# Queries turned by one transposing DMA instead of six fp32 TensorE products, for 12 of 16 head pairs

## The chip, the cores and the metric

The kernel runs on one core of a Trainium2 chip. The metric is the device time of one execution in microseconds (us); lower is better. Before the change it is 271.0 us, the median of three runs (269.58 to 273.28).

## The reference, cut to what matters

Two layers follow each other. The first is a block-sparse causal attention (4 batches, 8 heads, 768 positions, 64 wide): each query picks three key blocks of 64 by a gate score against the mean key of each block, and its own block. The second is a gated convolution over the sequence, done by FFT in the reference. Only the parts that the change touches are shown in full.

```python
# q, k, v: (4, 8, 768, 64) float32
k_rep = k.reshape(B, H, n_blocks, 64, D).mean(axis=3)
gate_scores = np.einsum('bhsd,bhnd->bhsn', q, k_rep)      # chooses the blocks
gate_scores = np.where(causal, gate_scores, -1e9)
top_idx = np.argsort(gate_scores, axis=-1)[..., -3:]       # plus the own block
scores = np.matmul(q, k.transpose(0, 1, 3, 2)) / np.sqrt(D)
attn = softmax(where(chosen_blocks & causal, scores, -1e9))
x = (attn @ v) as (4, 768, 512)

x1, x2, x3 = split(x @ w_proj)                             # 512 wide each
y = x1 * irfft(rfft(x2) * rfft(filter)) * x3
out = y @ w_out
```

The choice of blocks compares gate scores with each other, so it needs queries that are more exact than one rounding to 16 bits. The score product is content with the rounded ones.

## The kernel before

**Tiling.** Two heads of one batch form a pair `p` (0 to 15): 128 partitions of head dimension. The sequence is 6 chunks of 128. A pair has 6 slots of work, 3 per head, so there are 96 slots; pair `p` begins at slot `n0 = 6p`. In each slot the loop at L700 records, in this order: `scores` of the next slot (TensorE), `exponentials` of this slot (ScalarE, then a causal cut on GpSimd), the transfers gathered in `late` (`flush`), the list `early[n]`, a share of the second layer of the batch before (`hyena`), `products` of the slot before, and the list `bank[n]`. The schedule is written out by hand: every engine runs its instructions in the order in which they are recorded, and a waiting instruction holds all behind it on its engine. SyncE (SP) issues nearly all DMAs, also in that order, and it too stands still while one waits.

**What the queries need.** Their two heads are loaded side by side as fp32, positions on partitions (`q_nat`, three buffers). The products need them turned: 128 head dimensions on partitions, 768 positions along the row. Per pair `prep_q` (L325) is called twice, at slots `n0 - 9` and `n0 - 8`, each time for three chunks:

- `turned_pair` (L282): three fp32 products with an identity turn three chunks into a PSUM tile `qt` (L285). These tiles come from a pool of three (`one`), which most of the second layer's products use too.
- ScalarE rounds `32 q` to fp16 into `TQ` (L333). VectorE takes what the rounding left, `32 q - TQ`, as fp16 into `ql` (L335), without the first chunk, which needs no gate.
- After the second call a DMA copies the lower half of `TQ`, the second head, to `QB` (L339), as the score products of that head want it on partitions 0 to 63.

**Who uses them.** `prep_gate` (slot `n0 - 7`, L344 and L350): a bias product, then per chunk `TQ` twice and `ql` once against the two parts of the mean keys, 15 small products. `prep_mask` finds the third largest (VectorE). `prep_turn` (slot `n0 - 5`) turns the mask, ScalarE scales it (L383, tile `m`), and two DMAs put its rows at partitions 64 to 75 of `TQ` and `QB` (L385, L386), where the score product adds them. `scores` (L407) reads `TQ` with `KA` for the first head, `QB` with `KB` for the second.

**The other transfers of a pair on SP.** Loads of keys (`k_nat`, slot `n0 - 17`), queries (`n0 - 13`) and values (`n0 - 8`); the turned keys' halves to `KA` and `KB` (L307, L308); outputs (L576); and, for the second layer, one transposing DMA per pair from pair 4 on, except each batch's last pair (L455): it turns the attention's result `xnat`, six chunks of 128 x 128 in fp16, into `xT`.

**The second layer's inverse transform** keeps a tile `yy` per 128 channels (L544, four buffers).

Of the kernel before, what the change touches and what calls it, by code (L numbers as in the profile page):

```python
# [9 lines left out]
FP32 = mybir.dt.float32  # L10
FP16 = mybir.dt.float16
BF16 = mybir.dt.bfloat16
AF = mybir.ActivationFunctionType
ALU = mybir.AluOpType
# [4 lines left out]
def kernel(  # L19
# [10 lines left out]
    nc = tc.nc  # L30

    B, H, S, D = q.shape
    P = 128
    SC = S // P
    NB = S // 64
    Dm = H * D
    DC = Dm // P
    N3 = 3 * Dm
    F = 384
    HC = F // P  # L40
    NP = B * DC
    QS = 32.0
# [7 lines left out]
    fp = FP16  # L50
# [3 lines left out]
    const = ctx.enter_context(tc.tile_pool(name="const", bufs=1))  # L54
# [17 lines left out]
    nats = {}  # L72
# [94 lines left out]
    V16 = [const.tile([P, SC, 2, 66], fp, name=f"V16_{i}") for i in range(3)]  # L167
    KA = [const.tile([P, S], fp, name=f"KA{i}") for i in range(2)]
    KB = [const.tile([P, S], fp, name=f"KB{i}") for i in range(3)]
    TQ = [const.tile([P, S], fp, name=f"TQ{i}") for i in range(2)]  # L170
    QB = [const.tile([P, S], fp, name=f"QB{i}") for i in range(2)]
    id16 = const.tile([P, P], fp, name="id16")
    ownm = const.tile([P, SC - 1, 2, NB], fp, name="ownm")
# [150 lines left out]

    def prep_q(p, t):  # L325
        qn = nats["q", p]
        tq = TQ[p % 2]
        if t == 0:
            state["ql", p] = hp.tile([P, S], fp, name="ql", tag="ql")
        ql = state["ql", p]  # L330
        qt = turned_pair("qt", qn, t)
        cols = slice(F * t, F * (t + 1))
        nc.scalar.activation(tq[:, cols], qt, AF.Copy, bias=0.0, scale=QS)  # L333
        lo = P if t == 0 else 0
        nc.vector.scalar_tensor_tensor(out=ql[:, F * t + lo:F * (t + 1)], in0=qt[:, lo:F],  # L335
                                       scalar=QS, in1=tq[:, F * t + lo:F * (t + 1)],
                                       op0=ALU.mult, op1=ALU.subtract)
        if t == 1:
            late.append(lambda: nc.sync.dma_start(QB[p % 2][0:D, :], tq[D:P, :]))  # L339

    def prep_gate(p):
        tq, ql, kr = TQ[p % 2], state.pop(("ql", p)), state.pop(("kr", p))
        g = one("g", (P, SC - 1, 2, NB))
        nc.tensor.matmul(g.rearrange("p c h n -> p (c h n)"), lhsT=half1,  # L344
                         rhs=biasr.rearrange("p c h n -> p (c h n)"),
                         start=True, stop=False, skip_group_check=True)
        for c in range(1, SC):
            sl = slice(P * c, P * (c + 1))
            for lhs, rhs, last in ((tq, 0, False), (tq, 1, False), (ql, 0, True)):
                nc.tensor.matmul(g[:, c - 1], lhsT=lhs[:, sl], rhs=kr[:, rhs],  # L350
                                 start=False, stop=last, skip_group_check=True)
        state["g", p] = g
# [125 lines left out]
    def hyena(b, spread):  # L478
# [53 lines left out]
        def inverse(dc):  # L532
# [8 lines left out]
                                 start=(j == 0), stop=(j == HC - 1))  # L541
            yes = hy2.tile([P, F], FP32, name="yes", tag="yes")
            nc.scalar.copy(yes, ye)
            yy = hy.tile([P, 2, F], FP32, name="yy", tag="yy", bufs=DC)  # L544
            nc.vector.tensor_add(yy[:, 0, :], yes, yo)  # L545
            nc.vector.tensor_sub(yy[:, 1, :], yes, yo)  # L546
            st["y", dc] = yy
# [91 lines left out]
    def at(where, n, f):  # L639
        if n < slots:  # L640
            where[max(n, 0)].append(f)

    def gate_mask(p):
        prep_gate(p)
        prep_mask(p)

    for p in range(NP):
        n0 = 2 * NS * p
        k_at = {1: (0, 0), 2: (3, 3)}.get(p, (n0 - 12, n0 - 10))
# [2 lines left out]
        t_at = {1: 4, 2: 8}.get(p, n0 - 5)  # L652
        if p > 2:
            at(early, k_at[0] - 5, lambda p=p: load(p, "k"))
            at(early, q_at[0] - 4, lambda p=p: load(p, "q"))
        if p > 1:
            at(early, n0 - 8, lambda p=p: load(p, "v"))
        if p:
            for t in range(2):
                at(bank, k_at[t], lambda p=p, t=t: prep_k(p, t))  # L660
                at(bank, q_at[t], lambda p=p, t=t: prep_q(p, t))
            at(early, max(k_at[1] + 1, q_at[1]), lambda p=p: prep_kr(p))
            at(bank, g_at, lambda p=p: gate_mask(p))
            at(bank, t_at, lambda p=p: prep_turn(p))
            at(early, n0 - 3, lambda p=p: prep_v(p))
# [113 lines left out]
```

## Time and profile before

| | |
|---|---|
| median of three runs | 271.0 us (269.58 to 273.28) |
| the profiled execution | 272.46 us, its span 270.7 us, mean granted TensorE clock 0.979 |
| busy share of the span | TensorE 89%, VectorE 66%, ScalarE 63%, GpSimd 52% |
| fp32 products that turn the queries (L285) | 96, 17.4 us busy |
| rounding to `TQ` (L333) and the rest `ql` (L335) | 32 of 15.7 us and 32 of 15.5 us in total |
| transposing DMAs of `xnat` (L455) | 9 |
| DMA | 36.29 MB, 134 GB/s on the mean |

The span is what the profile covers, from the first to the last instruction; the 1.76 us around it belong to the time. Busy times of a group count overlapping instructions once. TensorE's products overlap each other by their latency, so a row of three products is busy for longer than it keeps the next one waiting. The profile's slices are 6.8 us each.

### The profile page before, as it was taken

Reading aid. Unit: us, or ns where it says so; the run is one execution under the profiler, and the core shown is the slowest. Engines: PE = TensorE matmul, PEld = TensorE weight load, DVE = VectorE, ACT = ScalarE, POOL = GpSimd, SP = SyncE. Lnnn points to the kernel's source line nnn. Section 1 sums busy time; section 2 is a strip of 40 time slices with the busy share of each in tenths; the row PEclk is TensorE's granted clock in tenths of the full one; section 3 lists DMA queues with packets and bytes.
Section 4 is the critical chain, followed back from the end, with each engine's and each line's share of the span. In section 5 each row is a group of like instructions: output and inputs, shape, how many; then the busy total and the mean of one; then the engine's idle time right before and its main releaser. Section 6 shows DMA issues by size and latency. Waiting matters only on the chain.

```text
span 270.7 us, 6236 instructions
## 1 busy us (share of the span) xinstructions
PE 242.0 (89%) x2228; PEld 150.3 (56%) x2228; DVE 179.1 (66%) x550; ACT 171.4 (63%) x275; POOL 140.9 (52%) x260
## 2 busy tenths in 40 slices
PE   7696869996999999989999999899999989897874
PEld 3365735565665667655656676566655654443431
DVE  3568658889477988654569885725698663256680
ACT  4567766774767577769764777797756756342333
POOL 7513342689635778653236876714277872006540
PEclk9999979997699999999999999999999999999999
DMA  8997977889797855677665467767241044200006
GB/s 162 209 153 208 245 205 140 157 162 212 128 190 159 155 124 131 125 210 232 150 134 121 106 150 105 190 212 195 59 93 37 1 33 155 77 2 0 0 0 232
DMA packets 93654, 36.29 MB, mean 134 GB/s; under 512 B 84292, under 2 KB 89784, under 8 KB 93624
## 3 DMA queue, kind: packets, MB, share of 16 engines
q1 hardware_dynamic: 91368, 33.81, 54.9%
q0 software_dynamic: 2256, 2.10, 5.9%
q8 instruction: 17, 0.28, 0.5%
q14 instruction: 13, 0.11, 0.2%
HBM read 24.64 MB, written 6.29 MB: 114 GB/s over the span
## 4 chain that ended last, share of the span: by engine, by line
PE 58%; DVE 15%; ACT 10%; POOL 6%; issue 4%; DMA 3%; SPq 1%; POOLq 0%; DVEq 0%; ACTq 0%
PE sps L407 8%; PE x2p L495 7%; PE op L572 6%; PE o L437 5%; PE x3p L560 5%; ACT ex L416 5%; PE x1p L557 4%; PE mt L371 2%; PE kt L285 2%; PE qt L285 2%; PE warm L92 2%; PE sps L557 2%; DVE xnat L446 2%; PE sps L560 2%; PE g L350 2%
## 5 line engine op out<-in xcount | busy, mean ns | idle before, releaser
L416 ACT ACTIVATE ex<-sps 128x896 f16<-128x896 f32 x96 | 88.3, 926 | 3.3 <-PE sps L407 3.0
L419 POOL TENSOR_SCALAR_AFFINE_SELECT ex<-ex 128x256 f16<-128x256 f16 x96 | 40.4, 424 | 82.6 <-ACT ex L416 78.3
L437 PEld LDWEIGHTS <-ex 128*128 128x128 f16 x672 | 32.7, 99 | 26.3 <-DVE xnat L446 11.6
L437 PE MATMUL o<-V,ex 128*128 128x65 f16 x672 | 37.5, 196 | 5.8 <-DVE xnat L446 4.4
L407 PE MATMUL sps<-QB,KB 76*128 76x512 f16 (+1 forms) x144 | 27.0, 297 | 3.7 <-ACT ex L416 3.6
L407 PE MATMUL sps<-TQ,KA 76*128 76x512 f16 (+1 forms) x144 | 27.4, 302 | 1.9 <-DMA QB<-m 1.3
L518 POOL TENSOR_TENSOR PQ<-ta 128x512 f16<-128x512 f32 x12 | 15.2, 1270 | 23.8 <-DVE ta L517 23.8
L572 PE MATMUL op<-wo,yT 128*128 128x512 f16 x96 | 24.2, 379 | 3.0 <-POOL yT L527 3.0
L301 DVE TENSOR_REDUCE krs<-kt 128x6 f32<-128x384 f32 x32 | 17.5, 553 | 13.5 <-ACT KH L298 13.3
L495 PE MATMUL x2p<-wp,xf 128*128 128x512 f16 x96 | 24.3, 379 | 0.8 <-DVE xf L474 0.8
L298 ACT CAST KH<-kt 128x384 f16<-128x384 f32 x32 | 15.2, 481 | 13.9 <-PE kt L285 12.6
L333 ACT ACTIVATE TQ<-qt 128x384 f16<-128x384 f32 x32 | 15.7, 495 | 12.3 <-PE qt L285 12.1
L335 DVE SCALAR_TENSOR_TENSOR ql<-qt,TQ 128x256 f16<-128x256 f32 (+1 forms) x32 | 15.5, 485 | 11.7 <-ACT TQ L333 11.6
L565 DVE TENSOR_TENSOR gg<-x1sb,x3p 128x384 f32<-128x384 f16 x24 | 13.2, 551 | 12.7 <-ACT x1sb L563 7.9
L527 POOL TENSOR_TENSOR yT<-gg,yy 128x384 f16<-128x384 f32 x16 | 15.9, 997 | 10.4 <-DVE yy L545 10.3
L575 ACT COPY osb<-op 128x512 f32<-128x512 f32 x24 | 14.1, 587 | 10.8 <-PE op L572 9.2
L560 PE MATMUL x3p<-xT,wp 128*128 128x384 f16 x96 | 19.6, 326 | 0.5 <-DVE yy L546 0.5
L407 PEld LDWEIGHTS <-KB 76*128 76x128 f16 x144 | 13.6, 100 | 11.0 <-issue 5.6
L557 PE MATMUL x1p<-xT,wp 128*128 128x384 f16 x96 | 19.5, 326 | 0.0
L383 ACT ACTIVATE m<-mt 44x768 f16<-44x768 f16 x14 | 11.3, 805 | 12.6 <-PE mt L371 12.6
L446 DVE TENSOR_TENSOR xnat<-o,rc 128x384 f16<-128x384 f32 x32 | 17.8, 558 | 1.1
L359 DVE MAX8 m<-g 128x8 f32<-128x12 f32 x160 | 13.9, 161 | 6.8 <-PE g L350 6.8
(155 smaller groups left out, 498.0 us busy)
## 6 DMA issues: line engine op xcount, KB each, us to landing
q_nat<-in_q_dram SPq DMA_DIRECT2D x32, 192.0 KB
k_nat<-in_k_dram SPq DMA_DIRECT2D x32, 192.0 KB
v_nat<-in_v_dram SPq DMA_DIRECT2D x32, 192.0 KB
out_dram<-osb SPq DMA_DIRECT2D x24, 256.0 KB
QB<-TQ SPq DMA_DIRECT2D x16, 96.0 KB
KA<-KH SPq DMA_DIRECT2D x16, 96.0 KB
KB<-KH SPq DMA_DIRECT2D x16, 96.0 KB
wp<-in_moe_w_proj_dram POOLq DMA_DIRECT2D x12, 128.0 KB, 3.8
```

The costliest lines, as they stand in the source:

```text
L301: nc.vector.tensor_reduce(out=krs[:, 6 * t:6 * t + 6], in_=kt.rearrange("p (n j) -> p n j", j=64), axis=AX.X, op=ALU.add)
L333: nc.scalar.activation(tq[:, cols], qt, AF.Copy, bias=0.0, scale=QS)
L407: nc.tensor.matmul(t[:, col:col + q1 - q0], lhsT=kk[0:64 + NB, P * kc:P * (kc + 1)], rhs=qq[0:64 + NB, q0:q1], start=True, stop=True, skip ...
L416: nc.scalar.activation(ex, t[:, 0:W], AF.Exp, bias=0.0, scale=EXPS)
L419: nc.gpsimd.affine_select(out=tri, in_=tri, compare_op=ALU.is_ge, fill=0.0, base=0, pattern=[[0, 2], [1, P]], channel_multiplier=-1)
L437: nc.tensor.matmul(o[:, qc, :], lhsT=ex[:, c0:c0 + P], rhs=V16[p % 3][:, kc, h, 0:65], start=first, stop=False, skip_group_check=True)
L446: nc.vector.tensor_tensor(xn[:, :, D * h:D * (h + 1)], o[:, :, 0:D], rc.to_broadcast([P, SC, D]), op=ALU.mult)
L495: nc.tensor.matmul(pa, lhsT=xf[:, eo, dc, P * i:P * (i + 1)], rhs=wp[:, dc, Dm:2 * Dm], start=(dc == 0), stop=(dc == DC - 1))
L527: nc.gpsimd.tensor_mul(st["yT"][:, dc, 0:F], g, yy[:, 0, :])
L557: nc.tensor.matmul(x1p, lhsT=wp[:, d2, dsl], rhs=xT[:, d2, hs], start=(d2 == 0), stop=(d2 == DC - 1))
L560: nc.tensor.matmul(x3p, lhsT=wp[:, d2, 2 * Dm + P * dc:2 * Dm + P * (dc + 1)], rhs=xT[:, d2, hs], start=(d2 == 0), stop=(d2 == DC - 1))
L572: nc.tensor.matmul(op, lhsT=st["yT"][:, cc, P * i:P * (i + 1)], rhs=wo[:, cc, :], start=(cc == 0), stop=(cc == DC - 1))
```

## The change

For pairs 4 to 15 `prep_q` is not called. In its place, taken straight from the loaded fp32 tile:

- `cast_q` (slot `n0 - 12`): one ScalarE instruction rounds `32 q`, 128 x 768, from SBUF into the first six chunks of a tile `q16`;
- `split_q` (`n0 - 11`): one VectorE instruction puts the rest of chunks 1 to 5, 128 x 640, into its last five;
- `send_q` (`n0 - 9`): one transposing DMA turns all eleven chunks, 128 x 1408 in fp16, into `TQL`, of which `TQ` and `QL` are two overlapping views;
- `part_q` (`n0 - 7`): the copy of the second head to `QB`, recorded in `early` and no longer in `late`.

The load of the queries of these pairs moves from slot `n0 - 13` to `n0 - 16`. Pairs 0 to 3 go on as before, into the same views. `ql` no longer has tiles of its own, and `yy` has three buffers instead of four.

```diff
-    TQ = [const.tile([P, S], fp, name=f"TQ{i}") for i in range(2)]
+    TQL = [const.tile([P, 2 * SC - 1, P], fp, name=f"TQL{i}") for i in range(2)]
+    TQ = [t[:, 0:SC, :].rearrange("p c s -> p (c s)") for t in TQL]
+    QL = [t[:, SC - 1:2 * SC - 1, :].rearrange("p c s -> p (c s)") for t in TQL]
...
     def prep_q(p, t):
         qn = nats["q", p]
-        tq = TQ[p % 2]
-        if t == 0:
-            state["ql", p] = hp.tile([P, S], fp, name="ql", tag="ql")
-        ql = state["ql", p]
+        tq, ql = TQ[p % 2], QL[p % 2]
...
+    def cast_q(p):
+        state["q16", p] = q16 = hp.tile([P, 2 * SC - 1, P], fp, name="q16", tag="q16")
+        nc.scalar.activation(q16[:, 0:SC, :], nats["q", p].rearrange("p c h d -> p c (h d)"),
+                             AF.Copy, bias=0.0, scale=QS)
+
+    def split_q(p):
+        q16 = state["q16", p]
+        nc.vector.scalar_tensor_tensor(out=q16[:, SC:2 * SC - 1, :],
+                                       in0=nats["q", p][:, 1:SC].rearrange("p c h d -> p c (h d)"),
+                                       scalar=QS, in1=q16[:, 1:SC, :],
+                                       op0=ALU.mult, op1=ALU.subtract)
+
+    def send_q(p):
+        nc.sync.dma_start_transpose(TQL[p % 2], state.pop(("q16", p)).rearrange("p c s -> p (c s)"))
+
+    def part_q(p):
+        nc.sync.dma_start(QB[p % 2][0:D, :], TQ[p % 2][D:P, :])
...
-            yy = hy.tile([P, 2, F], FP32, name="yy", tag="yy", bufs=DC)
+            yy = hy.tile([P, 2, F], FP32, name="yy", tag="yy", bufs=DC - 1)
...
+    TURNED = 4
...
-            at(early, q_at[0] - 4, lambda p=p: load(p, "q"))
+            at(early, q_at[0] - (7 if p >= TURNED else 4), lambda p=p: load(p, "q"))
...
-                at(bank, q_at[t], lambda p=p, t=t: prep_q(p, t))
+                if p < TURNED:
+                    at(bank, q_at[t], lambda p=p, t=t: prep_q(p, t))
+            if p >= TURNED:
+                at(early, n0 - 12, lambda p=p: cast_q(p))
+                at(early, n0 - 11, lambda p=p: split_q(p))
+                at(early, n0 - 9, lambda p=p: send_q(p))
+                at(early, n0 - 7, lambda p=p: part_q(p))
```

`q_at[0]` is `n0 - 9` for these pairs.

2 lines of the change are left out of this document (1 added, 1 removed).

## Prediction

> **What bounds the kernel now.** I read the page's totals and clock slices first, then busy time by stage, then the chain of waits in the steady stage.
>
> ```profile
> span 270.7 us, 6236 instructions
> ...
> PE 242.0 (89%) x2228; PEld 150.3 (56%) x2228; DVE 179.1 (66%) x550; ACT 171.4 (63%) x275; POOL 140.9 (52%) x260
> ...
> PEclk9999979997699999999999999999999999999999
> ```
>
> ```profile
> 61.50:65.00 3.50, 1.88 (x31) 1.45 (x30) 3.16 (x15) 1.41 (x3) 3.33 (x8) 0.99 1.01 224
> 65.00:68.40 3.40, 2.95 (x26) 2.12 (x24) 3.21 (x8) 1.66 (x3) 3.38 (x6) 0.50 1.23 224
> 66.00:103.90 37.90, 37.19 (x351) 24.52 (x352) 28.63 (x78) 25.89 (x42) 24.32 (x44) 0.92 0.82 157
> 103.90:159.50 55.60, 53.35 (x543) 34.68 (x540) 38.67 (x120) 40.32 (x67) 30.69 (x56) 1.00 0.63 150
> ```
>
> The columns of a stretch are: length, then busy time of TensorE, its weight loads, VectorE, ScalarE and GpSimd, then granted clock, DMA share, GB/s. From 66 us on TensorE is busy for 96 to 98% of the time: that is where the queries of pairs 7 to 15 are turned. Before 66 us it is not the bound (1.88 of 3.5 us), and the DMA engines are full there (shares 1.01 to 1.23). The chain of waits from 89.5 to 200.6 us says how much of the turning it holds:
>
> ```profile
> by line: PE sps L407 9.7%; PE x2p L495 9.3%; PE x3p L560 8.0%; PE op L572 6.9%; PE o L437 6.6%; ACT ex L416 6.5%; PE x1p L557 6.4%; issue 5.7%; PE qt L285 3.4%; PE kt L285 3.1%; PE mt L371 2.8%; PE xx L507 2.3%; PE g L350 2.3%; DVE gg L565
> ```
>
> **The saving.** A pair's query turning is two groups of three products. One of them, and what stands behind it:
>
> ```profile
> 99.75 0.53 PE L285 MATMUL qt<-id,q_nat 128*128 128x128 f32 x3
> 100.11 0.55 PE L407 MATMUL sps<-QB,KB 76*128 76x384 f16 x3
> ```
>
> A group holds TensorE for 0.36 us (99.75 to 100.11), a pair 0.72, twelve pairs 8.6. Not all of that arrives at the end: the chain holds `qt` for 3.4% of 111.1 us, 3.8 us for the 8 pairs in that stretch, or 0.47 each; elsewhere it runs through ScalarE, VectorE and issue, which don't get shorter. I take 0.47, so 5.6 us for twelve pairs, with 8.6 as the upper end.
>
> **ScalarE, VectorE, buffers.**
>
> ```profile
> L333 ACT ACTIVATE TQ<-qt 128x384 f16<-128x384 f32 x32 | 15.7, 495 | 12.3 <-PE qt L285 12.1
> L383 ACT ACTIVATE m<-mt 44x768 f16<-44x768 f16 x14 | 11.3, 805 | 12.6 <-PE mt L371 12.6
> L335 DVE SCALAR_TENSOR_TENSOR ql<-qt,TQ 128x256 f16<-128x256 f32 (+1 forms) x32 | 15.5, 485 | 11.7 <-ACT TQ L333 11.6
> L274 DVE SCALAR_TENSOR_TENSOR Asb<-hsb,tw,turn 128x512 f16<-128x512 f32 x3 | 2.6, 872 | 0.5 <-POOL turn L271 0.5
> 259.67 0.99 DVE L529 TENSOR_TENSOR yT<-gg,yy 128x384 f16<-128x384 f32 x1
> 260.58 0.54 DVE L545 TENSOR_TENSOR yy<-yes,sps 128x384 f32<-128x384 f32 x1
> ```
>
> ScalarE gives up two of 0.495 and takes one of 768 columns, 0.805 by the `m` row: 0.19 less per pair. VectorE gives up two of 0.485 and takes one of 640 columns out of SBUF: 0.81 by columns of the `ql` row (0.97 x 640/768), 1.09 by the `Asb` row, so -0.16 to +0.12 per pair. Both stand two slots or more ahead of their use, beside TensorE; ScalarE is busy for 40.32 and VectorE for 38.67 of 55.60 us. I cost them at nothing. Without that cover the cast would hold up the key casts behind it on ScalarE by 0.8 us per pair. The fourth `yy` tile now waits until the first one's `yT` is done: at the tail four tiles follow each other, the last written at 260.58, and even the third one's `yT` starts at 259.67 and ends within 0.1 us of it, the first one's about two rounds sooner. Nothing. Two PSUM tiles less per pair can only help a little.
>
> **The new path to the gate.** The transposing DMA is new work on SP, and the gate products now wait for its landing, with all of TensorE's queue behind them. SP's queue and TensorE around pair 8's gate:
>
> ```profile
> 94.02 1.25 SPq L455 DMA_TRANSPOSE xT<-xnat  x1
> 95.31 1.16 SPq L79 DMA_DIRECT2D k_nat<-in_k_dram  x2
> 96.58 0.80 SPq L385 DMA_DIRECT2D TQ<-m  x1
> 97.43 0.76 SPq L386 DMA_DIRECT2D QB<-m  x1
> 98.56 0.52 SPq L307 DMA_DIRECT2D KA<-KH  x1
> 99.12 0.59 SPq L308 DMA_DIRECT2D KB<-KH  x1
> 99.83 1.82 SPq L79 DMA_DIRECT2D v_nat<-in_v_dram  x2
> 102.76 0.47 SPq L339 DMA_DIRECT2D QB<-TQ  x1
> 103.27 1.25 SPq L79 DMA_DIRECT2D q_nat<-in_q_dram  x2
> ...
> 103.95 0.21 PE L344 MATMUL g<-biasr,half 128*128 128x120 bf16 x1
> 107.75 1.25 SPq L455 DMA_TRANSPOSE xT<-xnat  x1
> ```
>
> SP is nearly back to back from 94.02, when `xnat` frees it, to 99.71. The new transfer is issued behind `KB`, and the query load (1.25), which stood at 103.27, now stands ahead of `KA`. The 0.35 us that SP idles ahead of `KA` take up part of it, so `KB` ends 0.9 later. The gate stands 4.24 us behind the end of `KB`; less 0.9, and less the 0.72 by which TensorE comes sooner, 2.62 us are left. Is that enough? A transposing DMA with nothing beside it:
>
> ```profile
> L455 SPq DMA_TRANSPOSE xT<-xnat x9: 1243/1247/1330, 79.2 to 217.9; - x9
> 205.15 1.25 SPq L455 DMA_TRANSPOSE xT<-xnat  x1
> 206.15:206.35 0.20, 0.20 (x4) 0.08 (x2) 0.20 (x2) 0.20 (x1) 0.20 (x1) 1.00 0.00 0
> 206.35:207.35 1.00, 1.00 (x13) 0.63 (x12) 0.74 (x2) 0.98 (x2) 0.42 (x2) 1.00 0.98 193
> 207.35:207.55 0.20, 0.20 (x3) 0.14 (x2) 0.20 (x1) 0.20 (x1) 0.00 (x0) 1.00 0.10 17
> ```
>
> The first byte moves 1.2 us after the issue, then the engines are full for 1.0 us: six chunks have landed 2.3 us after the issue, or a little later. Eleven chunks move for 1.83. If the start stays at 1.2, they land after about 3.1 us; if the start grows with the size too, as the issue may, 2.2 + 1.83, say 4.15; never below the 2.3 of six. I take 3.1, as the first byte comes no later than the issue's end, so the transfer need not wait for a finished list. The Trainium skill ("DMA: Bandwidth & Descriptors", Latency and other measured facts) has 261 GB/s for a transposing DMA with a stride in the middle; by that eleven chunks (360 KB) would move in 1.4 us and land after 2.7. The trace's 193 GB/s speaks against it.
>
> The gate of pair 8 then waits 0.5 us. I let it stand for the seven pairs behind an `xT` transfer (7, 8, 9, 11, 12, 13, 15): 3.5 us. Two pairs (10, 14) have outputs ahead instead:
>
> ```profile
> 224.38 0.36 SPq L576 DMA_DIRECT2D out_dram<-osb  x1
> ...
> 124.73 0.78 SPq L386 DMA_DIRECT2D QB<-m  x1
> 125.61 1.39 SPq L576 DMA_DIRECT2D out_dram<-osb  x2
> 127.08 0.52 SPq L307 DMA_DIRECT2D KA<-KH  x1
> 127.66 0.59 SPq L308 DMA_DIRECT2D KB<-KH  x1
> ...
> 131.37 0.21 PE L344 MATMUL g<-biasr,half 128*128 128x120 bf16 x1
> ```
>
> Here 3.12 us lie between `KB` (ended at 128.25) and the gate. Two issues of 0.36 leave 0.67 of the 1.39 us for waiting, and 0.1 lies ahead of them, so of the load's 1.25 us 0.5 remain; less 0.72, 1.9 are left and the gate waits 1.2: 2.4 for two. Pairs 4 to 6, by pair 4:
>
> ```profile
> 47.31 0.59 SPq L308 DMA_DIRECT2D KB<-KH  x1
> ...
> 51.30 0.22 PE L344 MATMUL g<-biasr,half 128*128 128x120 bf16 x1
> ```
>
> Of 3.40 us the load takes 1.25 and the shorter TensorE queue 0.72; 1.43 are left, the wait is 1.7, and with full DMA engines not less: 5.1 for three. Waits in all 11.0.
>
> Behind the new transfer on SP stand the value load, needed five slots later (some 11 us at 13.7 per pair, 94.02 to 107.75, and six slots), and `part_q`, which waits for the landing at about 103.7, then the next `xT` at 107.75: 3 us of cover, nothing. The Trainium skill ("VectorE: DVE Perf Modes", The three transpose paths) speaks against the change: 1309 ns for one 128 x 128 by DMA against 390 on TensorE. By that, eleven chunks take 14.4 us; the trace has six landed in 2.3, so I don't use it.
>
> **The sum.** -5.6 + 11.0 = +5.4 us on the span of 270.7. On the profiled execution's own 272.46 (1.76 around its span) that is 277.9; from the median of 271.0, 1.5 lower, it is 276.4. I forecast 277.0, between the two.
>
> **Rivals.**
> - *The landing is hidden* (ends on the other side). If eleven chunks land in 2.3 us, pair 8's class waits nothing, pair 10's 0.4, pair 4's 0.9: 3.5 against 5.6 to 8.6 saved, so 265.9 to 268.9 from the median, say 267. It decides at 2.6 us. For it: first byte at the issue's end; against it: full engines for six chunks. Chance 0.20.
> - *The transfer moves at 1.4 us* (the page's rate, above), landing after 2.7: waits 0.1, 0.8 and 1.3, in all 6.2, which eats the saving: 271.6. Chance 0.10.
> - *The start grows with the size*: landing after 4.15, waits 1.5 (x7), 2.25 (x2), 2.7 (x3), 23.1 in all: 288.5. Chance 0.15.
> - *The clock.* At 61.5 us TensorE was busy for just over half of 3.5 us, and the clock fell to 0.50 for about one slice (6.8 us, the 7 and the 6 in PEclk). A gate wait of 1.6 us or more in a stretch with other gaps, likeliest at pairs 4 to 6, may do it again, for up to 3.4 us each; twice is 276 + 7 = 283. In the steady stage a wait of 0.5 is far from that. The Trainium skill ("TensorE: Matmul & The Clock Gate", Part 1) asks for a whole idle window of about 3.4 us; the row shows less sufficing. Chance 0.10.
> - *The change doesn't do what it says*: another path than described, no change. Chance 0.02.
>
> **The numbers.** The forecast (waits nearly as computed, 273 to 281, landing 2.9 to 3.4 us) has 0.43. About 2% (265.6 to 276.4) is what a measurement tells from no change here. Faster by more: a third of the first rival, where the whole 8.6 arrives and a little more, 0.07. Within: the rest of it (0.13), the rate (0.10), 0.02, and a bit under half of the forecast (0.19), 0.44. Slower: the other 0.24 and both slow rivals, 0.49. The range 266 to 285 leaves out the quickest end of the first rival and the slow start.
>
> **What would show it.** The gate's first product with `TQL` (after change) waits for a DMA in the list of waits, about 0.5 us for pairs 7 to 9 and over 1 us for 4 to 6, 10 and 14; transposing issues of two lengths, the new one 1.25 to 2.3 us; a period of the gates in the steady stage near 13.7 us, as before, not 13.0. I am wrong if TensorE never waits for that landing, or if the period shrinks by 0.7 us.

## The result and the profile after

| | before | after |
|---|---|---|
| median of four runs each, on one chip | 271.6 us (269.6 to 273.3) | 316.5 us (311.2 to 320.4) |
| ratio after to before | | 1.154, 95% interval 1.134 to 1.174 |
| the profiled execution, its span | 272.5 us, 270.7 us | 317.4 us, 315.6 us |
| mean granted TensorE clock | 0.979 | 0.910 |

Two of the four runs after, the profiled one among them, are over 1.5% above the fastest; the ratio compares the other two (311.2 and 315.7 us) with the four of before. The kernel became 15% slower, 45 us by the medians; the forecast was 277, its range ended at 285. The page of after, in the lines that answer to those shown of before (totals, clock slices, shares of the chain of waits, one group of instructions):

```profile
span 315.6 us, 6071 instructions
...
PE 250.0 (79%) x2156; PEld 150.1 (48%) x2156; DVE 181.4 (57%) x538; ACT 170.5 (54%) x263; POOL 144.6 (46%) x260
...
PEclk9997979697959869997969997989969999999998
...
DMA TQL<-q 19%; PE sps L426 9%; PE op L591 6%; PE x2p L514 5%; PE o L456 4%; PE x3p L579 4%; ACT ex L435 4%; PE x1p L576 4%; PE kt L288 3%; PE g L369 2%; PE mt L390 2%; PE xx L526 2%; PE warm L92 2%; PE sps L576 2%; PE sps L579 1%
...
L369 PE MATMUL g<-kr,TQL 128*128 128x24 f16 x240 | 9.3, 179 | 34.9 <-DMA TQL<-q 33.0
```

TensorE has 72 products less and is no longer the bound: a fifth of the chain (19% of 315.6, some 60 us) is now the transposing transfer. The gate products (L369) follow 33.0 us of idle time that this transfer ended, where the forecast had 11.0. And PEclk has sevens, sixes and a five up to the third quarter of the span; before, there were two such places.

The list of TensorE's waits for that transfer, over the whole span and for the pairs 8 to 14 alone (us in total, times, the longest):

```profile
PE g L369 <- DMA TQL<-q: 33.0, 11, 6.0
...
PE g L369 <- DMA TQL<-q: 13.2, 7, 3.3
```

So 13.2 us fall on seven pairs of the steady stage and 19.8 on pairs 4 to 7, while the projection's weights are loaded. Pair 15 does not wait. From the records of the single products and packets of after come, for each pair, when the last packet of its transfer ended (counted from the issue; called the landing below), and how long the gate stood between its bias product and its first product with `TQL` (from start to start, so 0.2 us longer than the wait in the list):

| pair | 4 | 5 | 6 | 7 | 8 | 9 | 10 | 11 | 12 | 13 | 14 | 15 |
|---|---|---|---|---|---|---|---|---|---|---|---|---|
| landing, us | 4.8 | 4.0 | 6.7 | 8.7 | 3.1 | 3.8 | 4.2 | 3.2 | 3.2 | 5.3 | 4.3 | 3.1 |
| wait, us | 5.6 | 3.4 | 5.5 | 6.2 | 0.8 | 1.5 | 3.0 | 0.8 | 2.5 | 2.5 | 3.5 | 0 |
| wait forecast | 1.7 | 1.7 | 1.7 | 0.5 | 0.5 | 0.5 | 1.2 | 0.5 | 0.5 | 0.5 | 1.2 | 0.5 |

Pair 10 in the timeline of after (start, us, engine or queue, line):

```profile
154.72 0.68 SPq L311 DMA_DIRECT2D KB<-KH  x1
155.49 1.50 SPq L355 DMA_TRANSPOSE TQL<-q  x1
157.08 1.87 SPq L79 DMA_DIRECT2D v_nat<-in_v_dram  x2
160.43 0.47 SPq L358 DMA_DIRECT2D QB<-TQL  x1
...
157.38 0.21 PE L363 MATMUL g<-biasr,half 128*128 128x120 bf16 x1
160.42 0.57 PE L369 MATMUL g<-kr,TQL 128*128 128x24 f16 x15 [2.82 <-DMA TQL<-q]
```

The issue takes 1.50 us, as forecast, and the gate comes 1.9 us behind it, also much as forecast. But gate and copy to `QB` are released only 4.93 us after the issue. What moved in between, by stretches of 0.5 us (busy time of the five engines, clock, DMA share, GB/s):

```profile
156.69:157.19 0.50, 0.50 (x4) 0.21 (x3) 0.00 (x0) 0.50 (x2) 0.00 (x0) 1.00 1.03 185
157.19:157.69 0.50, 0.41 (x9) 0.26 (x7) 0.00 (x0) 0.50 (x2) 0.09 (x1) 1.00 3.37 100
157.69:158.19 0.50, 0.00 (x0) 0.00 (x0) 0.00 (x0) 0.50 (x2) 0.32 (x1) 1.00 0.36 13
158.19:158.69 0.50, 0.00 (x0) 0.00 (x0) 0.00 (x0) 0.50 (x2) 0.00 (x0) 1.00 0.06 10
158.69:159.19 0.50, 0.00 (x0) 0.00 (x0) 0.00 (x0) 0.50 (x2) 0.29 (x1) 1.00 0.88 197
```

The transfer starts 1.2 us after its issue at 185 GB/s, as six chunks did. Then it stops: a DMA share of 3.37 in one stretch means packets that began there and lasted far beyond it, and for a microsecond 10 to 13 GB/s move. A stall within the transfer was in no part of the prediction.

The clock, by the periods that begin with the gates of pairs 8, 10 and 14 and over all seven up to the gate of pair 15; below it, for comparison, the same seven periods before:

```profile
126.70:141.00 14.30, 12.18 (x131) 7.83 (x127) 10.44 (x30) 9.37 (x16) 10.74 (x17) 1.00 0.72 136
157.40:176.40 19.00, 15.50 (x131) 9.06 (x127) 10.79 (x31) 9.38 (x15) 5.71 (x12) 0.82 0.64 122
225.60:244.90 19.30, 15.29 (x132) 9.02 (x129) 10.79 (x31) 9.39 (x15) 5.72 (x12) 0.82 0.58 92
...
126.70:244.90 118.20, 98.61 (x894) 59.94 (x891) 66.52 (x199) 70.36 (x108) 53.39 (x93) 0.90 0.72 142
```

```profile
103.90:200.60 96.70, 92.28 (x939) 60.07 (x936) 64.82 (x206) 70.53 (x115) 50.83 (x94) 1.00 0.63 150
```

Behind a wait of 0.8 us the clock stays at 1.00. Behind waits of 3.0 and 3.5 us it is 0.82 for 19 us, which is half the clock for 6.8 us.

It is not the length of a wait alone that decides. In these traces the granted clock changes on a grid of 3.41 us. Each of the five falls in the seven periods follows a cell of that grid in which TensorE is busy for 0.7 to 1.4 us; behind every other cell at full clock, with 2.3 us or more, it stays at 1.00. Shown are the cell of pair 9's wait (1.5 us) and the one behind it, then two cells of e8, an experiment below, whose gate of pair 14 waits for 3.1 us across both. The clock stays at 1.00 there, behind the second cell, too:

```profile
139.19:142.60 3.41, 0.72 (x12) 0.46 (x13) 0.61 (x2) 1.62 (x3) 2.69 (x6) 1.00 1.31 185
142.60:146.01 3.41, 3.41 (x30) 1.85 (x31) 1.40 (x13) 0.93 (x2) 0.26 (x1) 0.50 0.63 153
...
198.25:201.67 3.42, 1.59 (x16) 0.83 (x14) 0.00 (x0) 3.31 (x5) 0.82 (x3) 1.00 1.02 219
201.67:205.08 3.41, 2.31 (x33) 1.69 (x34) 1.67 (x13) 0.12 (x1) 0.00 (x0) 1.00 0.90 156
```

### The profile page after: what moved, and what is told of

Read it like the earlier page. It is cut to its first block, busy times and chain, and to the rows that moved or that the text cites. A ratio compares the mean times of both kernels' runs of the same rounds, so it can differ in the third digit from the quotient of the medians.

```text
span 315.6 us, 6071 instructions
## 1 busy us (share of the span) xinstructions
PE 250.0 (79%) x2156; PEld 150.1 (48%) x2156; DVE 181.4 (57%) x538; ACT 170.5 (54%) x263; POOL 144.6 (46%) x260
## 4 chain that ended last, share of the span: by engine, by line
PE 52%; DMA 21%; DVE 9%; ACT 8%; POOL 4%; issue 3%; SPq 1%; POOLq 0%; DVEq 0%; ACTq 0%
DMA TQL<-q 19%; PE sps L426 9%; PE op L591 6%; PE x2p L514 5%; PE o L456 4%; PE x3p L579 4%; ACT ex L435 4%; PE x1p L576 4%; PE kt L288 3%; PE g L369 2%; PE mt L390 2%; PE xx L526 2%; PE warm L92 2%; PE sps L576 2%; PE sps L579 1%
## 5 line engine op out<-in xcount | busy, mean ns | idle before, releaser
L438 POOL TENSOR_SCALAR_AFFINE_SELECT ex<-ex 128x256 f16<-128x256 f16 x96 | 44.5, 467 | 112.3 <-ACT ex L435 106.5
L456 PEld LDWEIGHTS <-ex 128*128 128x128 f16 x672 | 35.2, 103 | 27.9 <-DVE xnat L465 10.1
L456 PE MATMUL o<-V,ex 128*128 128x65 f16 x672 | 39.9, 202 | 5.1 <-DVE xnat L465 4.3
L378 DVE MAX8 m<-g 128x8 f32<-128x12 f32 x160 | 13.9, 160 | 47.7 <-PE g L369 47.7
L369 PE MATMUL g<-kr,TQL 128*128 128x24 f16 x240 | 9.3, 179 | 34.9 <-DMA TQL<-q 33.0
L426 PE MATMUL sps<-TQL,KA 76*128 76x512 f16 (+1 forms) x144 | 31.8, 339 | 3.5 <-DMA TQL<-m 2.7
L426 PE MATMUL sps<-QB,KB 76*128 76x512 f16 (+1 forms) x144 | 26.4, 291 | 6.3 <-ACT ex L435 5.9
L591 PE MATMUL op<-wo,yT 128*128 128x512 f16 x96 | 26.3, 403 | 4.2 <-POOL yT L546 4.2
L514 PE MATMUL x2p<-wp,xf 128*128 128x512 f16 x96 | 28.2, 425 | 0.8 <-DVE xf L493 0.8
L369 PEld LDWEIGHTS <-TQL 128*128 128x128 f16 x240 | 7.9, 101 | 37.0 <-DMA TQL<-q 34.6
L582 ACT CAST x1sb<-x1p 128x384 f16<-128x384 f32 x24 | 11.5, 480 | 23.0 <-PE x1p L576 22.7
L426 PEld LDWEIGHTS <-KA 76*128 76x128 f16 x144 | 14.0, 109 | 13.7 <-issue 5.5
L584 DVE TENSOR_TENSOR gg<-x1sb,x3p 128x384 f32<-128x384 f16 x24 | 13.2, 552 | 12.4 <-ACT x1sb L582 6.8
```

Source lines behind the costliest of these rows:

```text
L426: nc.tensor.matmul(t[:, col:col + q1 - q0], lhsT=kk[0:64 + NB, P * kc:P * (kc + 1)], rhs=qq[0:64 + NB, q0:q1], start=True, stop=True, skip ...
L438: nc.gpsimd.affine_select(out=tri, in_=tri, compare_op=ALU.is_ge, fill=0.0, base=0, pattern=[[0, 2], [1, P]], channel_multiplier=-1)
L456: nc.tensor.matmul(o[:, qc, :], lhsT=ex[:, c0:c0 + P], rhs=V16[p % 3][:, kc, h, 0:65], start=first, stop=False, skip_group_check=True)
L514: nc.tensor.matmul(pa, lhsT=xf[:, eo, dc, P * i:P * (i + 1)], rhs=wp[:, dc, Dm:2 * Dm], start=(dc == 0), stop=(dc == DC - 1))
L591: nc.tensor.matmul(op, lhsT=st["yT"][:, cc, P * i:P * (i + 1)], rhs=wo[:, cc, :], start=(cc == 0), stop=(cc == DC - 1))
```

## The experiments

Four theories stood at the start. **A**: traffic that is still moving right ahead of the transfer in SP's queue (the query load, moved there by the change, and the copies to `KA` and `KB`) stalls it, and the clock falls behind the waits. **B**: the transfer itself, by its size, is what costs. **C**: the earlier query load hurts by what it delays. A fourth, about the clock, says that it only accompanies the waits. Each kernel was timed beside the kernel before on the same chip, which took 270.5 to 271.2 us there (medians). Diffs are against after where nothing else is said. A time from one run is less sure than the medians: the four runs of after differ by 9 us.

### Parts of the change alone: e4, e1, e2, e3

**e4**, the kernel before with the moved load alone:

```diff
-            at(early, q_at[0] - 4, lambda p=p: load(p, "q"))
+            at(early, q_at[0] - (7 if p >= 4 else 4), lambda p=p: load(p, "q"))
```

> The kernel before with one thing of the change alone: the query load at n0 - 16 instead of n0 - 13 for pairs 4 to 15. Theory A: the load hurts only because the transposing transfer stands behind it, so 271 within 4 us. Rival C: 285 or more, with waits behind KA and KB, which the load now delays.

One run: 272.9 us. C falls, which said 285 or more: the load alone costs no more than the runs of before differ among themselves.

**e1**, the transfer sent one slot earlier:

```diff
-                at(early, n0 - 9, lambda p=p: send_q(p))
+                at(early, n0 - 10, lambda p=p: send_q(p))
```

> The transposing transfer is issued one slot earlier, so that the query load and the copies to KA and KB stand behind it on SP's queue and no longer right ahead of it. Theory A (packets of the load and copies right ahead, still moving when the transfer starts, stall it; the clock then falls after each wait): the gates wait for less than 8 us in all instead of 33, the time is 265 to 280. Rival B (the transfer is slow by itself, or its bytes are too many for the DMA engines): still 300 or more, since about 2 us of lead per pair are bought, 24 of 33 us of waits go at most, and the packets last as long as before. Rival C (the load of the queries three slots earlier is what hurts, through what it delays): still 295 or more, since the load stays where it is.

One run: 275.8 us, at a clock of 0.963. From pair 7 on every landing is 3.0 us (pair 9: 3.2), and only two gates still wait, in the stretch of the weight loads. Lines of its list of waits (for `TQL` and, new, the cast of the queries for their load):

```profile
ACT q L344 <- DMA q_nat<-in_q_dram: 6.2, 2, 3.3
...
PE g L369 <- DMA TQL<-q: 1.9, 2, 1.2
```

One line gives back most of the 45 us: 41 by this run, 36 by the median of four runs of the same kernel (e12). That is what A said; B and C said 295 or more.

**e2**, the load three slots earlier still:

```diff
-            at(early, q_at[0] - (7 if p >= TURNED else 4), lambda p=p: load(p, "q"))
+            at(early, q_at[0] - (10 if p >= TURNED else 4), lambda p=p: load(p, "q"))
```

> The query load is issued three slots earlier still (n0 - 19), so that only the copies to KA and KB stand right ahead of the transposing transfer. Theory A: the transfer lands some 3 us after its issue at the pairs behind the projection's weight loads (pairs 8 to 15), as it did at pair 15, the only one with no load ahead; gate waits of 4 to 12 us in all, 268 to 282. Rival B: 305 or more. Rival C (an early query load hurts whatever stands behind it): 305 or more, too; it differs from B in the landing, which would then be 3 us.

One run: 286.6 us, above A's 268 to 282. From pair 8 on six of eight landings are 3.1 us, as expected, but pairs 10 and 14 land after 4.2, and the gates wait 13.9 us in all. With an undisturbed landing of 3.1 us they are released 4.0 us after the issue in the plain cases (pairs 8 and 12): the last packet is not the end of the transfer for the engine that waits.

**e3**, twelve products of zeros (128 x 512) in front of the gate's products, so that TensorE has work while it waits:

```diff
+        if p >= TURNED:
+            busy = one("busy")
+            for _ in range(12):
+                nc.tensor.matmul(busy, lhsT=zeros[:, 0:P], rhs=zeros, start=True, stop=True,
+                                 skip_group_check=True)
```

> Twelve extra products of zeros (128 x 512, about 0.22 us each, 2.6 us) stand ahead of the gate's products for pairs 4 to 15, so that TensorE stays busy for most of the wait. Their time lies in the wait as far as that reaches. If the granted clock's fall after the waits is a large part of the loss: the clock's mean rises from 0.910 to 0.95 or more, and the time falls to 290 to 308, although work was added. If the clock is only a companion of the waits: 316 or more (the waits are as before, and where one is shorter than 2.6 us the products add to it).

One run: 309.2 us, just beyond the 290 to 308 of "the clock matters" (the mean clock is 0.976, as that expectation had it), and 7 us faster than the median of after in spite of 144 more products. The steady stage tells it better. The seven periods from the gate of pair 8 on, in e3:

```profile
124.60:237.20 112.60, 105.86 (x975) 63.63 (x974) 66.45 (x199) 69.39 (x106) 53.83 (x92) 1.00 0.71 149
```

The clock is 1.00 throughout, and 112.6 us are less than the 118.2 of after, although 84 products of 0.217 us (18.2 us) stand where after waits 13.2. Undisturbed, these periods take 94.4 us (e1 and e17): 94.4 + 18.2 = 112.6, as measured. In after 94.4 + 13.2 leaves 10.6 us, and a clock of 0.90 over 118.2 us is 11.8 us of clock lost. So in the steady stage the waits cost nearly as much again through the clock as by themselves.

### Which neighbour stalls the transfer: e6, e7, e8, e5

**e6**, the load behind the transfer instead of ahead:

```diff
-            at(early, q_at[0] - (7 if p >= TURNED else 4), lambda p=p: load(p, "q"))
+            at(early, q_at[0] - (6 if p >= TURNED else 4), lambda p=p: load(p, "q"))
```

> After, with the query load one slot later (n0 - 15): on SP's queue it then stands right behind the transposing transfer of the pair before and no longer right ahead of it; the copies to KA and KB stay ahead. Theory A (a load still moving when the transfer starts stalls it): the last packet comes about 3.1 us after the issue at the pairs from 8 on, as for the eight pairs of the early-load kernel with only the copies ahead; the gate is released about 0.9 us behind that, so it waits for 0 to 1.5 us a pair from pair 8 on, 8 to 20 us in all, and the time is 278 to 292. Rival D (the copies to KA and KB ahead stall it as much as the load): waits stay near 33 us, 308 or more.

One run: 302.4 us, in neither band. From pair 8 on four landings are 3.1 to 3.2 us and four (9, 10, 13, 14) 4.1 to 4.7. A had no room for those. The waits of e6 show a second loss besides, which A did not have either:

```profile
ACT q L344 <- DMA q_nat<-in_q_dram: 30.6, 9, 6.7
...
PE g L369 <- DMA TQL<-q: 21.2, 10, 5.3
```

A load behind the transfer comes too late for the cast, and ScalarE stands still for it, with the exponentials behind.

**e7**, six chunks only; the rest is left out, and the gate uses old values for it:

```diff
-        nc.sync.dma_start_transpose(TQL[p % 2], state.pop(("q16", p)).rearrange("p c s -> p (c s)"))
+        nc.sync.dma_start_transpose(TQL[p % 2][:, 0:SC, :],
+                                    state.pop(("q16", p))[:, 0:SC, :].rearrange("p c s -> p (c s)"))
```

> After, but only the six chunks of the rounded queries are turned by the transfer (768 packets instead of 1408); the five chunks of the rest are left out, and the gate uses old values for them. The query load stays right ahead. Theory A (the stall is that of a transposing transfer started while the load moves, whatever its size): the stalls stay, with packets that take 0.4 us or more at most pairs; the landing comes 0.8 us earlier with each, so the waits are 33 - 12 x 0.8 = 23 us or a little less, 298 to 310. Rival B (the size is what hurts): the waits fall below 8 us, 265 to 280.

One run: 299.9 us, waits of 22.5 us, both as A said. B falls: with little over half the packets the stalls are still there (landings of 2.4 to 2.5 us at pairs 8, 11, 12 and 15, 3.1 to 3.9 at 10, 13 and 14).

**e8**, the new path from pair 8 on (`TURNED = 8`), and **e5**, the same with the transfer sent one slot earlier as in e1:

```diff
-    TURNED = 4
+    TURNED = 8
```

> After, with the new path from pair 8 on only (TURNED = 8), so that no transposing transfer of queries falls in the stretch in which the projection's weights are loaded (pairs 4 to 7). If the collision with the weight loads makes the loss: within 4 us of 271. If the query load ahead on SP's queue makes it and the weight loads only add to it: 285 to 296, since in the trace of after the gates of pairs 8 to 15 span 118.2 us where they spanned 97 before, 21 us more, and the gate of pair 8 was 23 us late.

> Both mends: the transfer is issued one slot earlier, ahead of the load and the copies, and the new path begins with pair 8. In the early-send kernel the gates from pair 7 to 15 span 108.5 us where they span 111.1 before, and the loss of 5.8 us came up to pair 7. Theory A: 267 to 270, about 1% faster than before, a period of 13.2 to 13.5 us instead of 13.7. If the early-send kernel's loss at pairs 4 to 7 comes up elsewhere instead: 272 or more.

e8: one run, 287.7 us, within the second band. So pairs 4 to 7, with the weight loads, hold 29 of the 45 us by this run, the steady stage the rest. e5: median 273.2 us of ten runs, ratio 1.008 (1.003 to 1.013): A's 267 to 270 is missed. Landings: 4.2, 3.9, 3.8, 3.2, 4.3, 3.8, 3.5 and 4.3 us, seven of eight stalled, with only two copies of 18 KB right ahead. And from pair 8 on e5 has the very instructions around each transfer that e1 has, where nothing stalled. That is the end of A as the whole cause. In e5 no gate waits for `TQL` by the list any more; it is the query load, issued behind the stalled transfer, that comes late for ScalarE's cast:

```profile
ACT q L344 <- DMA q_nat<-in_q_dram: 3.5, 3, 1.6
```

### Behind, chance, or something else: e12, e9, e10, e11

Rival **F**: what is issued right behind the transfer stalls it. **e12** is e1 once more; **e9** and **e10** are e1 with `TURNED` 7 and 6; **e11** is e5 with `part_q` at slot `n0 - 10`, so that SP stands still until the landing.

> The early-send kernel once more, in three rounds. Two questions. Is the stall inside the transposing transfer a matter of chance? If it is fixed by the program, the landings of pairs 8 to 15 are again 3.0 us after the issue but for pair 9 (3.2), and the time is 274 to 278; if it is chance, two to six of these eight land after 3.7 us or more, as seven of eight did in the kernel with both mends, which issues the same instructions around them. And the interval against the kernel before: 1.00 to 1.03.

> Send early, new path from pair 7 on. From pair 8 on every engine does what it does in the early-send kernel (landings 3.0 us, no stalls) and in the one that begins with pair 8 (landings 3.2 to 4.3, seven of eight stalled); the three differ in how many packets went through the queue before. If that number decides: a pattern of its own, the same kind for most of the eight pairs. If traffic right ahead decides (theory A): 3.0 for all, as nothing but two copies of 18 KB stand ahead. Time 268 to 274 in either case.

> The same, from pair 6 on: as for the kernel from pair 7 on. Time 268 to 276.

> The kernel with both mends, with the copy to QB issued right behind the transposing transfer. It waits for the landing, so nothing else can be issued behind the transfer while it moves. If what is issued right behind makes the stalls (rival F): landings of 3.0 us for all eight, where they were 3.2 to 4.3. If not: still above 3.7 for most. The load and the copies to KA and KB then come 3 us later; time 269 to 275.

e12: median 280.9 us, ratio 1.026 (1.014 to 1.037), slower than the 274 to 278 expected, so e1 does not beat the kernel before either. Landings of pairs 8 to 15 are again 3.00 to 3.05 us: the stall is not chance. The time is less fixed: of the 9.0 us between the traces of e1 and e12, 5.1 lie ahead of pair 8's gate and 3.9 in the period behind it. e9: one run, 277.4 us, above the 268 to 274 expected, two of eight stalled (pairs 9 and 13, 4.2 and 4.0); e10: one run, 273.4 us, one stalled (pair 13, 4.2). e11: all eight land after 3.1 us, as F said, but one run gives 332.2 us, for a reason of its own. The copy now stands ahead of the last score products of the pair two before, which use the same buffer; these read the new queries, and wait for them:

```profile
PE sps L426 <- DMA QB<-TQL: 49.5, 8, 7.2
```

### Neighbours taken away one by one: e14, e15, e13, e16

The same experiment without that fault: behind the transfer SP copies 128 bytes out of `TQL`, which holds it until the landing. **e14** is after with this fence, **e15** is e1 with it, **e13** is e5 with it. **e16** is after with the transfer issued on ScalarE's own queue.

```diff
         nc.sync.dma_start_transpose(TQL[p % 2], state.pop(("q16", p)).rearrange("p c s -> p (c s)"))
+        nc.sync.dma_start(rest, TQL[p % 2][0:1, 0, 0:64])
```

> After, with that small copy behind the transfer and nothing else changed: the query load and the copies to KA and KB stay right ahead, the value load now waits behind the landing. Rival F: landings of 3.0 to 3.3 us from pair 8 on, waits of the gate 0.5 to 1.0 us a pair there and 2 to 3 at pairs 4 to 7, 10 and 14, 14 to 22 us in all, 283 to 297. Theory A (the load right ahead makes it): landings of 3.8 us or more at most pairs, as in after, waits of 28 to 36 us, 308 or more.

> The early-send kernel (from pair 4 on) with the small copy behind the transfer: nothing of size ahead, nothing behind. Landings of 3.0 to 3.1 us from pair 7 on by both theories; in the stretch of the weight loads, up to pair 7, 3.3 us or more, since those come by another queue. The query load behind it comes 2 us later, and the cast waits for it there. 271 to 280.

> The kernel with both mends (sent one slot earlier, from pair 8 on), with a copy of 128 bytes out of the turned tile issued right behind the transposing transfer. It waits for the landing, so SP issues nothing while the transfer moves; the copy to QB stays where it was. Rival F (what is issued right behind makes the stall): landings of 3.0 to 3.1 us for all eight, where the kernel with both mends had 3.2 to 4.3, periods of 13.2 to 13.6 us, and 266 to 270. If the stall does not come from behind: landings above 3.7 for most, 271 to 275.

> After, with the transposing transfer issued by ScalarE on a queue of its own instead of by SP, at the same slot. It no longer stands behind the load and the copies, so it starts 2 to 4 us earlier against the gate, and has no neighbours in its queue; ScalarE pays 1.4 us of issuing per pair, 12 times, which its idle time covers. If neighbours in the queue make the stall: landings of 3.0 to 3.3 us, waits below 6 us in all, 266 to 278. If the traffic on the engines itself makes it: landings of 3.7 us or more at many pairs in spite of that; the waits still fall, as it starts earlier, to 8 to 20 us, 278 to 295.

e14: one run, 308.7 us, five of the eight landings from pair 8 on at 4.1 to 5.0, gate waits 28.4 us, all as A said. e15: one run, 300.2 us, all eight at 3.0 to 3.1. e13: 287.7 us, ratio 1.058 (1.045 to 1.071), seven of eight at 3.6 to 4.4, with nothing behind and nothing of size ahead. F falls with e13. Both times lie far above their bands, as in e13 and e15 the fence keeps the load back; the row of e13:

```profile
ACT q L345 <- DMA q_nat<-in_q_dram: 22.2, 7, 4.5
```

e16: one run, 280.1 us, clock 0.969; gate waits 5.8 us. The transfers now have a queue of their own (q10), in which their packets stand alone. At pairs 4 to 6 they land after 4.4 to 6.3 us, and from pair 8 on after 3.3 to 4.5, seven of eight after 3.7 or more. So the order in SP's queue is not needed for a late landing. Beside each of these eight, 60 to 340 KB move on SP's queue (q1), the query load among them; the DMA view around pair 8's transfer, from its issue at 106.28 to its landing (window 106.3 to 110.6):

```profile
q1 hardware_dynamic: 1627, 0.47, 46.2%
q10 hardware_dynamic: 1436, 0.36, 45.8%
```

The landings and the time are those of "the traffic on the engines itself", the waits those of the other half of the expectation, as the transfer starts earlier.

### The packet that the stall waits for: e17, e18

With no load ahead or on another queue (e1, e5, e9, e10, e13) the pattern goes by kernel, not by neighbours. What coincides with a stall in each of these traces is a packet on another queue: instructions. The DMA view of e5 (shares in 40 slices of the window, then the queues) around pair 9's transfer, issued at 110.84:

```profile
DMA  0903799999999999999900000011001010010101
...
q1 hardware_dynamic: 530, 0.14, 109.0%
q8 instruction: 1, 0.02, 3.9%
```

The window is 111.9 to 113.9. The transfer runs for 0.9 us, then nothing moves, and one packet of queue 8 lies in the window. The kernel before had it, too, around its last transfer of `xnat`, at 217.87 (window 219 to 221), with nothing else issued on SP between 208.4 and 224.3 us:

```profile
DMA  0199999999999999999000000000000000010000
...
q1 hardware_dynamic: 515, 0.13, 137.8%
q8 instruction: 1, 0.02, 4.9%
```

The page of after on queue 8 (packets, MB, share):

```profile
q8 instruction: 17, 0.28, 0.4%
```

That is 16 KB each, for 2156 products and as many weight loads, one for every 254 instructions of TensorE, so about one for every pair. Where it falls against the transfer depends on how many instructions came before; that is what `TURNED` changes. **e17** (on e5) and **e18** (on after) shift it alone: the warm-up products at the start are cut into eight parts each, 84 more products with 84 weight loads.

```diff
-    def warm(n):
+    def warm(n, parts=1):
...
-            nc.tensor.matmul(t, lhsT=zeros[:, 0:P], rhs=zeros, start=True, stop=True,
-                             skip_group_check=True)
+            for j in range(parts):
+                cols = slice(512 // parts * j, 512 // parts * (j + 1))
+                nc.tensor.matmul(t[:, cols], lhsT=zeros[:, 0:P], rhs=zeros[:, cols], start=True,
+                                 stop=True, skip_group_check=True)
...
-    warm(3)
+    warm(3, 8)
```

> The kernel with both mends (sent one slot earlier, from pair 8 on), with the warm-up products at the start cut into eight parts each: 84 more products with their weight loads, 168 instructions of TensorE, some 8 us of its stream in the steady stage. If the instruction fetch makes the long stall: the fetches fall 5 to 8 us ahead of the transfers, all eight land 3.0 to 3.2 us after the issue where seven of eight landed after 3.4 to 4.3, periods are 13.2 to 13.6 us except one of 14.1 per batch, and the time is 266.5 to 270.5, ratio 0.985 to 1.00. If it does not: landings above 3.4 us as before, 272 to 275.

> After with the same 84 additional products at the start, nothing else. In the trace of after the landings of 3.8 us or more from pair 9 on (pairs 10, 11, 14 and, with a smaller packet, one more) have a fetch inside them, and pair 5. If the fetch makes them: from pair 9 on landings of 3.0 to 3.4 us, waits of the gate 5 to 8 us less in all and fewer slices at half clock, 298 to 312; what is left comes from the load ahead, the weight loads at pairs 4 to 7 and the release behind the last packet. If not: 313 to 320.

(In the second, "pairs 10, 11, 14" should read 10, 13 and 14.) e17: median 268.8 us of twelve runs, ratio 0.990 (0.986 to 0.994). No 16-KB packet lies near a transfer any more, and all eight land after 2.99 to 3.06 us. Pair 9's transfer of e17, issued at 111.18, in a window at the same distance (112.25 to 114.25), and the seven periods from the gate of pair 8 on:

```profile
DMA  0013899999999999999999999999999999999978
...
q1 hardware_dynamic: 1492, 0.37, 97.5%
```

```profile
103.10:197.50 94.40, 87.81 (x895) 55.30 (x891) 65.67 (x199) 70.37 (x108) 54.19 (x94) 1.00 0.81 179
```

84 products that compute nothing make the kernel 4 us faster by the medians. In e5 these periods take 97.1 us, and the cast's wait for its load, shown above, is gone from the list of e17. e18: one run, 308.5 us, gate waits 26.4 us instead of 33.0, the seven periods 112.2 us instead of 118.2; the mean clock is 0.908, no better than in after. From pair 8 on the landings are 3.05 to 3.7 us, with one of 4.1, where an instruction packet of 8 KB lies inside. So the fetch is some 8 of the 45 us of after, by one run that lies 3 us below the lowest of after's four.

Over the 16 kernels with all eleven chunks on SP's queue, pairs 8 to 15, that is 128 transfers: 34 have a 16-KB instruction packet that begins between 0.2 us ahead of the issue and 2.9 us behind it, and all 34 land after 3.45 us or more, up to 5.3. (With one that begins at 2.95 us, pair 12 of after lands after 3.2.) Of 84 without any instruction packet in that time the middle one lands after 3.06 us and 78 within 3.35; the other six, 3.4 to 3.8, are in kernels with the query load or outputs ahead (e3, e8, e18). In 10 cases only an 8-KB packet lies inside: 3.0 to 4.1.

## Why the prediction was wrong

**What held.** TensorE's bound and the saving: 94.4 us instead of 96.7 for seven periods (e17) is 0.33 us a pair, where 0.47 was forecast. ScalarE's and VectorE's new instructions, and the fourth `yy` tile, cost nothing: from the gate of pair 15 to the end it is 70.1 us before, 70.7 after, 70.4 in e1. From pair 8 on the length of the issue, its place behind `KB`, the 1.2 us to the first byte and the rate held: 1408 packets of 256 bytes in the 1.8 us from 1.2 to 3.0 are 200 GB/s, by the rows of six chunks 193. (The Trainium skill, "DMA: Bandwidth & Descriptors", Latency and other measured facts, has 261 for one with a stride in the middle; no run here comes near it.) The gate waits where the forecast looked for it, and longer at pairs 4 to 6, 10 and 14, as it said; but pair 7, put at 0.5 us, waits longest, and pair 15 not at all.

**The step that failed** is the term "landing", in the words of the prediction "I take 3.1", from which all waits of the gate were worked out; and the clock behind these waits, which the sum put at nothing, took 10.6 us in the seven periods. Four things are missing from the 3.1:

- The last packet lands after 3.0 to 3.1 us when undisturbed, exactly as computed, but the waiting engine is released later: 4.0 us after the issue in e2. Those 0.9 us alone would turn the 0.5 us of pair 8's class into 1.4. The prediction had "or a little later" for it and counted nothing.
- The instruction fetch stalls the transfer by 0.4 to 2.2 us, some 8 us of the total by e18's one run. The prediction used one of nine transfers of `xnat` (205.15) and called it one "with nothing beside it". The last of the nine landed after 3.9 us.
- At pairs 4 to 7 the bounds were carried over from the quiet stage, "with full DMA engines not less". There the waits were 19.8 us, not 5.6: 1024-byte packets of the weight loads share the engines, and pair 7 landed after 8.7 us. e8 shows the size: by its one run, 29 us of the loss go with these four pairs.
- The query load right ahead costs as well: with it, landings without a fetch are 3.1 to 3.7 us (after, e18), without it 3.0 to 3.1 (e15, e17). With its packets beside the transfer on another queue it is 3.3 to 4.5 (e16). It was moved there by the change; the prediction counted its 1.25 us of SP's time, but not its packets. The copies to `KA` and `KB` alone cost 0.1 to 0.2 (six pairs of e2, 3.06 to 3.12, and pair 7, 3.2).

**The rivals.** "The landing is hidden" and "1.4 us" had the kernel faster or unchanged. "The start grows with the size" came nearest in time (288.5, chance 0.15): its landing of 4.15 us is near the release that the gate saw without stalls (4.0 to 4.1 at pair 8 of after and of e2). That is luck: its reason is wrong, as the first byte comes at 1.2 us, and its 17.5 us are less than half of the loss. **The clock** (0.10) was the right mechanism, and "1.6 us or more in a stretch with other gaps" fits the trace of after: waits of 1.5 us and more brought it, those of 0.8 did not. It was put at pairs 4 to 6 and kept out of the steady stage, as "a wait of 0.5 is far from that"; with waits of 1.5 to 3.5 us it came there at five gates of seven. The length alone is no rule in the other traces. Waits of 1.8 us (e2, pairs 10 and 14) and 3.1 us (e8, pair 14) left the clock at 1.00, one of 1.0 us with other gaps around it (e18, pair 13) did not: what counts is how little TensorE does in one cell of the grid. The Trainium skill ("TensorE: Matmul & The Clock Gate", Part 1) has a whole idle window of about 3.4 us for the fall; here a cell with 0.7 to 1.4 us of work in it suffices, and the fall then lasts for 3.4 us or 6.8.

The sum for the steady stage, seven periods: forecast -3.3 (7 x 0.47) + 4.9 (waits of pairs 8 to 14) = +1.6 us. Measured +21.5 (118.2 less 96.7): -2.3 saved, +13.2 waits, +10.6 the clock. Up to the gate of pair 8 the loss is 22.8 us (126.7 against 103.9), where the forecast had about +3.2 (5.6 of waits less five pairs' 2.4).

**What stays open.** How the instruction packet holds the transfer up, and why the release trails the last packet by 0.6 us in one pair and by 2.2 in another (pair 12 of after), was not settled. A 16-KB packet begins at 2.95 us in pair 12, just as the last packets move, but at 3.19 in pair 11, where the release trails by 0.6. Where half the clock begins between 1.4 and 2.3 us of work in a cell, these traces do not show sharply: one cell of e8 with 1.8 brought the fall, one with 1.6 did not. That queue 8 serves TensorE is inferred from its count and from e17 and e18. e17's gain of 1% holds for the place at which its fetches happen to lie; a change in the number of products ahead of it would move them again.

## What to carry to other kernels

When a transfer takes the place of engine work, cost it by the release of the engine that waits, not by its last packet, and take the worst of all like transfers in the trace rather than the tidiest; then ask who else moves packets at that time, queues of other engines and instruction fetches among them. Give it slack of the whole spread: here 3.0 us of packets, 0.9 of release and up to 2.2 of stall, where 1.4 to 2.6 us were left. A wait on TensorE has two prices, its length and the clock behind it. The second falls due when TensorE does too little in one cell of the clock's grid; in after that was so behind waits of 1.5 us and more, and in its steady stage the two prices were nearly equal.

## What the runs showed of the hardware

- **An instruction fetch stops a transposing DMA.** One 16-KB packet on the instruction queue inside the transfer: landing 3.45 to 5.3 us instead of 3.0, 34 times out of 34; moved away by 84 idle products, 0 of 8. In the view of pair 10 above, 10 to 13 GB/s are left during the stall. The Trainium skill ("Runtime: NRT & Kernel Launch", Instruction fetch mechanics) states blocks of 16 KiB, 256 instructions, which the 254 of the page bear out. It calls the cost of crossing a block mostly hidden; for a transposing transfer beside it, with 0.4 to 2.2 us, it is not.
- **The place of an instruction in its stream is a resource.** From pair 8 on e5 and e17 differ in nothing but 168 instructions at the start: 1.008 against 0.990.
- **Waiting can be dearer than working.** e3 does 18.2 us of useless products in the steady stage and is faster there than after by 5.6 us, since the clock stays up.
- **Traffic of another queue stretches the transfer, too.** On a queue of its own, with 60 to 340 KB moving on SP's queue meanwhile, it lands after 3.3 to 4.5 us (e16, pairs 8 to 15, with no 16-KB instruction packet inside).
- **The clock is judged cell by cell.** On a grid of 3.41 us, a cell with 0.7 to 1.4 us of work on TensorE was followed by half the clock in after; 3.1 us of waiting split over two cells, with 1.6 and 2.3 us of work, left it at 1.00 in e8.
